# A two-block kernel under a new written order: every engine's queue, the buffer slots and the filler matmuls exchanged

## The chip, the cores and the metric

The kernel runs on one core of a Trainium2 chip. A core has TensorE (matrix products into the accumulator memory PSUM; "PE" in the profile, its weight loads "PEld"), VectorE (DVE), ScalarE (ACT), GpSimd (POOL) and SyncE (SP), which here only issues DMA transfers; ScalarE and GpSimd issue some too. Every engine works through its own queue strictly in the written order and waits at semaphores for the others. The metric is the device time of one execution in microseconds (us); lower is better.

## The reference

Attention with sketched polynomial features for 4 batches, 4 heads, 1088 tokens and head size 32, and then a token-mixing block over the heads joined to 128 channels:

```python
a, b = einsum('rd,bhsd->bhsr', S1, x), einsum('rd,bhsd->bhsr', S2, x)
phi(x) = einsum('bhsi,bhsj->bhsij', a, b)              # 8 x 8 = 64 features
num = phi(q) @ (phi(k)^T v);  den = phi(q) @ sum(phi(k)) + 1e-06
x = num / den                                          # joined: (4, 1088, 128)
theta = x @ w_theta;  zr, zi = x * cos(theta), x * sin(theta)
u = x + w_tok_r @ zr + w_tok_i @ zi                    # w_tok_*: 1088 x 1088
out = u + maximum(u @ w_ch, 0)
```

## The kernel before

The kernel does not issue its work in the order in which its source describes it. The source declares 1022 operations, numbered 0 to 1021 in the order of the calls of `op` (`vop`, `small` and `join` call it too). Each names its engine ("P" TensorE, "V" VectorE, "A" ScalarE, "G" GpSimd, "S" SyncE), what it reads and writes, and holds a function that issues one or many instructions. `Layout.run` then takes the order from the string `ORDER`, a permutation of the 1022 numbers, and a slot for every buffer from the string `PLACES`. `Layout.issue` issues them one after the other, so an engine's queue is the subsequence of `ORDER` that belongs to it. `SPINS` says ahead of which operations how many filler matmuls go (`spin`, line 379: 384 columns of zeros, into a bank that nobody reads). The classes of buffers are in the table `classes`: 22 big ones, 5 of class "zs" for raw weight rows and for z, 8 PSUM banks, and smaller ones. Two buffers in the same slot follow one another: the first operation of the later one waits for all users of the earlier one. All waits follow from the data and the slots.

The stages, with the numbers that the text uses (b is the batch, g a group of three 128-token chunks, of which each batch has three):

- *Start*: fillers (1), constants (2), a dummy sine `warm` (3, line 384), the sketch matrices and their scaling (5 to 43; 7 is ScalarE's Prelu at line 412, 16 its scaling at lines 469 to 471, 17 VectorE's rounding; 41 and its GpSimd products 42 and 43 belong to a product of the two sketches; 31 builds the blocks that the first product of the chain takes). Loads on SyncE: k 44, 47, 48, 49, q 45, 50, 51, 52, v 46, 53, 54, 55 for batches 0 to 3, a second copy of k for batches 2 and 3 (56, 57), and w_theta with w_ch (58).
- *Keys and chain* (58 to 304): transposes of k, features, outer products on VectorE and products with v (of batch 2, the third outer product is 207 and its product 208), a Gram matrix of k, and a chain of tiny operations that makes scales and sliced feature matrices.
- *Queries* (305 to 334): transposes and slices of q; 328 and 329 are the correction of batch 2's q, which GpSimd adds by an accumulating DMA.
- *Weight rows* (335 to 419): 17 rows of 128 x 1088 eight-byte words arrive in "zs" slots and are unpacked: five operations a row, a load (SyncE), two activations (ScalarE, lines 584 and 586), a shift and an addition (VectorE, lines 309 and 305). Row i has the numbers 335 + 5i to 339 + 5i; row 13's addition is 404 and row 16's 419.
- *Per batch* (420 on): "levels" (products of q with the feature matrices, lines 987 to 1005), "den" (VectorE), "num" (outer product, transposition, product, copy into xT), "theta" (products with w_theta; ScalarE turns the phase with lines 1111 to 1117, three of which are Abs and two sines; VectorE subtracts at line 312 and multiplies into z at line 305). For batches 2 and 3 transpositions go through memory: VectorE turns blocks of 32, SyncE and ScalarE scatter them (line 333), SyncE fetches them back.
- *Mixing*: batch 0 takes all three column spans of a row in one operation (482 to 498, row 16 in 498), batch 1 one span at a time (579 to 641). Batches 2 and 3 share seven half-size products, `winograd` (787 to 1006), which need sums of weight rows (line 305, 128 x 544) and differences of z (835 for the first). Then the output product and the store.

In theta of batch 0, 468 and 460 are VectorE's subtractions for groups 1 and 0, 459 is ScalarE's copy ahead of 460, and 469 to 471 are the Abs and the two sines of group 1. In theta of batch 2, 695 and 717 are VectorE's products into z of groups 0 and 2; 815 and 793 are the first matmuls that need them. The num products of batch 3 are 740, 747 and 754; the scatters that ScalarE issues for it are 738, 745 and 752.

Of the kernel before, what the change touches and what calls it, by code (L numbers as in the profile page):

```python
# [26 lines left out]
TINY = 2.0**-60  # L27
UP = 256.0
ORDER = (
# [37 lines left out]
)  # L67
PLACES = (
# [8 lines left out]
)  # L77
SPINS = (
    "70:2 15:3 137:1 211:1 424:2 128:1 168:1 174:2 176:1 521:2 "
)  # L80
WARM = 0
SPLIT = ()
# [1330 lines left out]
```

## Time and profile before

| | |
|---|---|
| median of 3 runs (lowest, highest) | 219.07 us (218.96, 219.25) |
| profiled execution, first to last instruction | 217.4 us; the page gives no other time of it |
| TensorE busy | 209.3 us (96%), 1998 matmuls |
| VectorE busy | 181.2 us (83%) |
| ScalarE busy | 111.2 us (51%) |
| GpSimd busy | 22.2 us |
| DMA | 40.58 MB, mean 187 GB/s; over 290 GB/s in most of the first 100 us |
| granted TensorE clock | 0.997 of full speed |

Busy times are unions of rows, and the rows of matmuls overlap in the pipeline: a row of 0.27 us can be followed by the next after 0.11 us. Where an operation's price is meant, the time from start to start says more. An engine that is not the bottleneck may stand idle at no cost, so what matters is which engine has no room in which stretch of the span.

### The profile page before, as it was taken

What the parts mean: (1) busy time and instruction counts of PE and PEld (TensorE: products, weight loads), DVE (VectorE), ACT (ScalarE), POOL (GpSimd) and SP (SyncE); (2) the same over time, 40 slices, a digit from 0 to 9 for tenths busy, and PEclk for the clock granted to TensorE, in tenths of its full rate; (3) what the DMA queues carried; (4) which work ended last, traced back from release to release, by engine and by line L of the source; (5) the groups of instructions that cost most, each with busy time, mean ns of one, the idle gap of its engine ahead of it and who ended that gap; (6) DMA issues with size and microseconds to landing.
All of it is one profiled execution on the core that took longest, in us unless ns stands there. A gap on an engine that the chain in (4) does not pass through costs nothing.

```text
span 217.4 us, 5063 instructions
## 1 busy us (share of the span) xinstructions
PE 209.3 (96%) x1998; PEld 154.3 (71%) x1998; DVE 181.2 (83%) x408; ACT 111.2 (51%) x214; POOL 22.2 (10%) x44
## 2 busy tenths in 40 slices
PE   7999899999999999999999999999999999999994
PEld 3987786686766686666766575667758788888883
DVE  4899999999999999999599839988138999996542
ACT  3998498899779999983322040354037400000010
POOL 2237000055000000100132000100101000000000
PEclk9999999999999999999999999999999999999998
DMA  5999996869979979894226998599911000045253
GB/s 153 429 406 340 425 399 203 333 224 271 267 276 361 361 264 380 219 198 126 33 36 102 222 137 199 105 156 151 231 78 32 0 0 0 3 66 89 36 79 75
DMA packets 52635, 40.58 MB, mean 187 GB/s; under 512 B 45444, under 2 KB 47108, under 8 KB 50436
## 3 DMA queue, kind: packets, MB, share of 16 engines
q1 hardware_dynamic: 35540, 33.71, 48.7%
q0 software_dynamic: 1728, 4.65, 10.5%
q10 hardware_dynamic: 15344, 1.90, 6.0%
q8 instruction: 15, 0.25, 0.5%
q14 instruction: 8, 0.07, 0.1%
HBM read 30.43 MB, written 5.18 MB: 164 GB/s over the span
## 4 chain that ended last, share of the span: by engine, by line
PE 72%; DVE 12%; ACT 8%; DMA 4%; ACTq 2%; issue 2%; SPq 1%
PE ps L341 66%; DMA big<-q_l 2%; DVE lv L305 2%; PE ps L1064 2%; ACTq L333 2%; PE ps L1098 1%; DMA fx<-g 1%; DVE g L305 1%; DVE big L305 1%; PE ps L967 1%; ACT big L584 1%; ACT big L937 1%; DVE hf L309 1%; DVE zs L305 1%; ACT g L1068 1%
## 5 line engine op out<-in xcount | busy, mean ns | idle before, releaser
L341 PE MATMUL ps<-big,zs 128*128 128x384 f32 (+4 forms) x398 | 109.7, 424 | 0.4 <-DVE zs L305 0.4
L341 PEld LDWEIGHTS ps<-big,zs 128*128 128x128 f32 x398 | 71.4, 190 | 30.3 <-issue 2.6
L1201 ACT COPY g<-ps 128x128 f32<-128x128 f32 (+1 forms) x3 | 0.9, 301 | 42.5 <-PE ps L1193 42.5
L305 DVE CUSTOM_DVE_ANT_0 big<-big,big 128x2176 uint16<-128x2176 uint16 x17 | 21.8, 1287 | 0.4 <-ACT big L586 0.2
L584 ACT ACTIVATE big<-zs 128x1088 f32<-128x1088 f32 x17 | 20.9, 1235 | 2.1 <-DMA zs<-w_tok 1.2
L586 ACT ACTIVATE big<-zs 128x1088 int32<-128x1088 uint32 (+1 forms) x18 | 21.3, 1184 | 0.1
L341 PE MATMUL ps<-big,big 128*64 128x64 f32 (+2 forms) x208 | 20.6, 276 | 0.0
L341 PEld LDWEIGHTS ps<-big,big 128*64 128x64 f32 (+1 forms) x208 | 16.5, 154 | 2.9 <-issue 0.2
L305 DVE TENSOR_TENSOR big<-big,big 128x544 f32<-128x544 f32 x24 | 16.7, 712 | 0.0
L1002 ACT COPY lv<-ps 128x480 f32<-128x480 f32 x12 | 6.3, 563 | 14.2 <-PE ps L341 14.2
L312 DVE SCALAR_TENSOR_TENSOR g<-g,ps 128x384 f32<-128x384 f32 x12 | 6.6, 548 | 8.1 <-ACT g L1111 8.1
L1078 ACT COPY big<-ps 128x384 f32<-128x384 f32 x12 | 5.9, 489 | 14.0 <-PE ps L341 8.3
L309 DVE TENSOR_SCALAR big<-big 128x1088 int32<-128x1088 int32 x17 | 12.2, 724 | 0.6 <-ACT big L584 0.5
L341 PEld LDWEIGHTS ps<-w,big 128*128 128x128 f32 x80 | 10.6, 192 | 2.3 <-ACT g L1068 0.6
L319 POOL DMA_DIRECT2D big<-hf x6 | 5.4, 957 | 63.3 <-DVE g L312 33.8
L319 POOL DMA_DIRECT2D g<-big x6 | 5.2, 920 | 64.8 <-ACT g L1179 34.7
L341 PE MATMUL ps<-w,big 128*128 128x128 f32 x80 | 11.8, 280 | 0.0
L305 DVE TENSOR_TENSOR g<-lv 128x768 f32<-128x768 f32 x12 | 11.2, 945 | 0.0
L341 PE MATMUL ps<-g,sm 128*64 128x384 f32 x48 | 10.1, 507 | 0.2 <-ACT big L1078 0.2
L305 DVE TENSOR_TENSOR zs<-ps,g 128x768 f32<-128x768 f32 (+2 forms) x15 | 9.4, 632 | 1.0 <-PE ps L1098 0.9
L341 PEld LDWEIGHTS <-hf 128*64 128x64 f16 (+1 forms) x288 | 7.7, 110 | 2.9 <-issue 1.7
L379 PE MATMUL ps<-idle 128*128 128x384 bf16 x27 | 7.8, 400 | 1.3 <-POOL idle L381 1.3
(194 smaller groups left out, 336.6 us busy)
## 6 DMA issues: line engine op xcount, KB each, us to landing
zs<-w_tok SPq DMA_DIRECT2D x17, 1088.0 KB, 7.0
big<-k_l SPq DMA_DIRECT2D x6, 576.0 KB, 6.6
big<-hf POOLq DMA_DIRECT2D x6, 576.0 KB, 6.0
big<-v_l SPq DMA_DIRECT2D x4, 576.0 KB, 7.0
g<-fq SPq DMA_DIRECT2D x6, 384.0 KB, 5.2
big<-q_l SPq DMA_DIRECT2D x3, 576.0 KB, 5.1
fq<-g SPq DMA_DIRECT2D x12, 96.0 KB, 4.0
fq<-g ACTq DMA_DIRECT2D x12, 96.0 KB, 4.1
```

Source lines behind the costliest of these rows:

```text
L305: eng.tensor_tensor(out=o, in0=a, in1=b, op=f)
L309: (eng or V).tensor_scalar(out=o, in0=a, scalar1=s1, scalar2=s2, op0=op0, **kw)
L312: (eng or V).scalar_tensor_tensor(out=o, in0=a, scalar=s, in1=b, op0=op0, op1=op1)
L319: op("G", 0.9, lambda: G.dma_start(dst(), src(), accum_op=ALU.add), w, r, fly=fly)
L333: E.dma_start(there().rearrange("(a i) (x b j) -> b i x a j", a=nf, b=nf, j=SQ)[f], blocks()[f * SQ:(f + 1) * SQ].rearrange("i (x a j) -> ...
L341: T.matmul(o, lhs, rhs, start=start, stop=stop, skip_group_check=True)
L379: T.matmul(nowhere() if home is None else view(home, (GW,), F32), idle()[:, 0:P], idle(), start=True, stop=True, skip_group_check=True)
L584: op("A", 0.22 + n * 0.0009, lambda: A.activation(dfn(), words_of(raw(), n)[1].bitcast(F32), AF.Prelu, scale=2.0**-112, alpha=-(2.0**32)), ...
L586: op("A", 0.22 + n * 0.0009, lambda: A.activation(stp(), words_of(raw(), n)[0].bitcast(U32), AF.Copy, scale=2.0**-29), [stp], [raw])
L1002: op("A", act(480), lambda g=g, lp=lp: A.copy(lv().rearrange("p l (c n) -> p l c n", n=HR)[:, :, g * GC:(g + 1) * GC], lp().rearrange("p c ...
L1064: T.transpose(tr()[:, i * P:(i + 1) * P], qp()[:, i * H + 2 * n:i * H + 2 * n + 2].rearrange("p h i j -> p (h i j)"), ident())
L1078: op("A", act(GW), lambda g=g, xp=xp: A.copy(xt()[:, g * GW:(g + 1) * GW], xp()), cells(xt, g * GW, (g + 1) * GW), [xp])
```

## The change

Three strings are exchanged, `ORDER`, `PLACES` and `SPINS`. The operations, their functions and all that is computed stay the same, and so does the number of buffer slots of each class. What differs is the sequence of every engine's queue, which buffers share a slot, and where how many fillers go. The diff, cut to the lines of the new strings that the text speaks of (the old `ORDER` begins with the two lines shown):

```diff
 ORDER = (
-    "6 4 2 5 44 0 1 45 50 3 47 7 340 8 48 46 11 9 10 49 12 29 58 13 30 70 83 84 64 76 71 14 77 85 96 15 88 72 89 78 "
-    "65 86 90 97 79 16 91 66 159 17 92 26 87 98 67 148 27 93 80 32 18 68 19 73 99 309 25 94 141 20 310 74 95 31 142 "
...
+    "4 5 6 7 2 8 9 44 11 10 0 1 12 70 13 83 14 15 71 47 64 16 129 58 84 85 88 89 65 135 29 30 45 26 17 18 90 130 131 66 "
+    "49 21 148 151 40 41 43 132 50 59 61 91 152 92 48 136 153 133 93 19 86 149 96 150 97 94 95 20 159 355 98 87 101 67 "
+    "60 102 305 99 306 160 161 340 103 137 162 138 68 104 22 23 72 73 154 246 25 74 42 309 310 31 105 139 307 36 35 106 "
...
+    "354 387 518 216 520 437 438 523 465 524 525 217 439 453 467 254 255 468 147 440 454 386 256 199 441 469 526 470 471 "
+    "241 527 528 529 455 188 200 456 360 189 442 530 531 361 532 466 242 533 457 459 460 51 473 475 257 267 540 536 218 "
...
+    "404 495 569 556 416 417 243 649 557 294 558 559 418 419 299 496 497 3 498 295 296 560 511 512 499 561 625 626 505 "
...
 SPINS = (
-    "70:2 15:3 137:1 211:1 424:2 128:1 168:1 174:2 176:1 521:2 "
+    "70:1 113:1 233:2 126:1 448:2 189:2 536:2 "
 )
```

Read by engine: SyncE's queue begins with 6, 44, 45, 50, 47, 340, 48, 46, 49, 58 before, and with 6, 44, 47, 58, 45, 49, 50, 48, 355, 340 after. The dummy sine 3 is ScalarE's second entry before; after, it follows the second sine of theta in batch 1, group 0 (559), behind the unpacking of row 16 (416, 417). The last two weight rows in VectorE's queue are 13 and 16 after; they were 15 and 16 before. The fillers of the first product (operation 1, ten of them) and the one of operation 128 stay.

80 rows, old and new, of tables (ORDER, PLACES) are left out of this document.

## The prediction

> **What bounds the kernel now.** First the table of busy time by stretch of the span (start:end and length in us, then busy us and instructions of TensorE, its weight loads, VectorE, ScalarE and GpSimd, the granted clock, the DMA engines' share, GB/s).
>
> ```profile
> 0.00:24.00 24.00, 21.94 (x367) 17.27 (x367) 19.77 (x83) 19.24 (x48) 8.58 (x29) 1.00 0.88 341
> 24.00:60.00 36.00, 34.17 (x595) 26.20 (x595) 35.69 (x88) 30.45 (x59) 5.95 (x5) 1.00 0.89 296
> 60.00:100.00 40.00, 39.34 (x311) 26.64 (x311) 38.85 (x66) 36.13 (x56) 0.85 (x1) 1.00 0.86 280
> 100.00:145.00 45.00, 44.71 (x396) 28.71 (x394) 35.66 (x73) 11.92 (x24) 5.10 (x7) 1.00 0.66 126
> 145.00:170.00 25.00, 24.91 (x118) 18.66 (x119) 15.25 (x30) 11.65 (x25) 1.71 (x2) 1.00 0.57 120
> 170.00:200.00 30.00, 30.00 (x134) 24.82 (x133) 28.24 (x55) 0.87 (x2) 0.00 (x0) 1.00 0.16 26
> ```
>
> From 24 to 100 us VectorE is busy for 74.5 of 76 us: nothing can be put in there. From 100 us on it has room (35.7 of 45, 15.3 of 25) and TensorE has none. Then VectorE's waits between 24 and 102 us, which are all that the view lists:
>
> ```profile
> DVE big L309 <- ACT big L584: 0.5, 2, 0.3
> DVE big L305 <- ACT big L586: 0.2, 1, 0.2
> ```
>
> So there are two stages: until the last token-mixing row is unpacked VectorE sets the pace, and afterwards TensorE works off what is left. The hinge shows in the timeline (start, length, instruction; the last unpacking on VectorE) and in the chain that ended last (TensorE's long pieces):
>
> ```profile
> 98.63 1.29 DVE L305 CUSTOM_DVE_ANT_0 big<-big,big 128x2176 uint16<-128x2176 uint16 x1
> ```
>
> ```profile
> 83.10 44.99 PE ps L341 x362
> ...
> 145.07 21.94 PE ps L341 x102
> ...
> 172.89 37.32 PE ps L341 x170
> ```
>
> Last the rows of two things that the change moves, from the groups (busy us, mean ns, then the idle time ahead and what ended it):
>
> ```profile
> L379 PE MATMUL ps<-idle 128*128 128x384 bf16 x27 | 7.8, 400 | 1.3 <-POOL idle L381 1.3
> L384 ACT ACT_TABLE_LOAD x1 | 1.3, 1283 | 1.6 <-DVE hm L366 1.6
> ```
>
> **How I count.** An operation's price is the time from its start to the next start on its engine, where that one waited for nothing (rows overlap by some 0.1 us, so row lengths would count too much). Added so, VectorE has 181.2 us of work, ScalarE 127 with its DMA issues, and TensorE 198.2 without fillers. A filler between others starts 0.163 us ahead of the next. Adding the prices in the written order gives the work that stands ahead of each operation in both kernels; clock time less this sum is what an engine has lost.
>
> Before: up to the end of row 16's unpacking (operation 419) VectorE has 94.9 us of work; the clock says 99.92, so 5.0 are lost, 3.0 of them by 13.7 us, while the first loads arrive, and the rest in drips. Its matmuls (498) start at 100.18. From there TensorE has 111.1 us of work and ends at 213.98: 2.7 lost, of which 0.45 is the wait for zs at 144 us and the rest switches between kinds of matmul, 0.05 to 0.1 us each. The last instruction ends 3.4 us later: 100.2 + 111.1 + 2.7 + 3.4 = 217.4, the span. The page gives no other time of the profiled execution; the median of the runs, 219.07, is 1.67 above the span, and I carry that over.
>
> **The change, part by part.** No operation comes or goes, so nothing is won from work except fillers: 16 become 11, 5 x 0.163 = 0.8 us. Those of before stand partly in waits, and so do the new ones (ahead of 113, 448, 189 and 536, each of which waits for VectorE), so the saving lies between 0 and 0.8; it is contained in the TensorE sums below.
>
> *Which VectorE operation is the last that TensorE must wait for.* In the new order it is the outer product 207 (batch 2, third group): VectorE's work up to its end is 86.5 us, and TensorE's work from its user 208 to the end is 121.3. Together 207.8, against 94.9 + 111.1 = 206.0. Nearly as tight is row 13 (404 for 495: 91.7 + 116.0 = 207.7). So the new order holds TensorE back at a point where it has 10 us more to do: +1.8 us.
>
> *The start.* On SP's queue k of batch 1 moves from fifth to third, ahead of both q, and row 1 behind k of batches 2 and 3. Before, k0 landed at 5.36, q0 at 7.15, q1 at 8.57 and k1 at 9.99, so k1 should land at about 7 and q0 at 9.2. The scaling of the small matrices (16, 17), late by ScalarE's place in the queue (8.8 us), follows k0's first copy at 6.6. Following VectorE's queue with these times I find nothing it waits for between 6 and 24 us, and a loss of 2.1 at 14 us in place of 3.0: -0.9 us. Bounds: 0 (the load comes no earlier) and -1.5. The drips (1.7 us from 14 to 87 us) I leave as they were. POOL's queue has the small product 43 ahead of the slices; it waits for 41 at about 10.4, and what is behind it (31, wanted at 15.9) ends at about 13.4.
>
> *The table load.* Operation 3, the dummy sine, goes from the head of ScalarE's queue to row 16's end. The one load row stands ahead of it, and it is the kernel's first function. The new first function is the Prelu of 7, and the first sine is 470 (theta, batch 0, group 1). Whether a Prelu's table holds a sine no row shows: a second load costs ScalarE between 0 and 1.28 us, and I take 1.28, as the one load that shows belongs to a sine. Does VectorE feel it? 469 ahead of it waits for VectorE's 468. From 469 to the end of 459 ScalarE has 4.7 us of work; VectorE, from the end of 468 to 460, which needs 459, has 4.9. With the load, 6.0 against 4.9: VectorE stands for 1.1 us, in the full stage and ahead of 207. Without it the cover is 0.2.
>
> [...]
>
> *Behind 100 us.* The three num products of batch 3 (740, 747, 754) now follow each other, which saves about two pairs of switches, 0.4 us; the 0.45 wait should go, as 695 ends some 1.4 us ahead of 815. But theta2_2 now ends just as its user 793 is due (both at about 154), behind ScalarE's scatter issues for batch 3 (738 and 752: 2.2 and 1.3 us on ScalarE), and zc1 (835) ends 0.3 us ahead of 846. For these I take 0.5 us (0, if they hold, to 2, if the issues are as slow as the slowest pair, 3.5 us). 2.7 - 0.4 - 0.4 + 0.5 = 2.4.
>
> *Slots.* Row 16's raw slot is freed by row 12's second activation (397) at about 89.7; with its 7.0 us to land, ScalarE has it at 96.7, and VectorE wants it at 98.4. The q2 correction (POOL, 329) leaves at 81 and lands in 6.3 us; its user 652 is due at 88.9. Covers of 1 to 2 us: no cost, and all of a delay beyond them.
>
> Sum: 86.5 + (2.1 + 1.7 + 1.1 lost) + 121.3 + 2.4 + 3.4 = 218.5, 1.1 above 217.4; 219.07 + 1.1 = **220.2 us**.
>
> **Rivals.** (1) *Faster: VectorE loses less ahead of 207.* If ScalarE keeps a lead over VectorE all along (at 460 too), the start's 2.1 and 0.5 of drips remain, 2.6 instead of 4.9: 216.2, or 217.9 in the runs. For it: the waits above, the only ones listed for the full stage, are for ScalarE's unpacking (0.7 us), and by the sums the new order has that unpacking 8 to 10 us of VectorE work earlier. Against: the cover of 0.2 at 460. It decides below a loss of 3.8. (2) *No second load, or it is covered:* 217.4, no change, 219.1. For it: ScalarE has idle time; against: the count above. (3) *A load or a round trip is late* at one of the covers of 1 to 2 us: row loads took up to 11 us among others (row 13), 4 more than I allow, so 2 to 3 us more: 222.5.
>
> **Chances.** Forecast 0.48, rival 1 0.28, rival 2 0.1, rival 3 0.14. 0.2% (0.4 us) is about what these runs can tell from no change. Of the forecast's share a little falls within that, of rival 2's a third on each side: faster 0.33, same 0.12, slower 0.55. Alone the forecast has 219.3 to 221.3. The range takes in rival 1's 217.9 with 1.2 us for more of the start and the fillers, and rival 3's 222.5: 216.7 to 222.6.
>
> **What the profile after would show.** A second ACT_TABLE_LOAD row at about 49 us on ScalarE, and VectorE waiting for L1111 some 1 us there: if the row is absent, that step is wrong. k1 landed near 7 us and VectorE's work 0.9 us further at 14 us. TensorE waiting for VectorE at L341 (kv, batch 2) near 91 us, and 498 starting after 101. Waits for zs (theta2_2) near 154 would show the tight second stage. I am wrong if VectorE shows other waits of a microsecond between 24 and 95 us, or none.

## The result, and the profile after

The changed kernel takes 226.38 us (median of 4 runs, 225.89 to 228.12), against 219.16 us for the kernel before beside it: 1.0324 times as long, 95% interval 1.0274 to 1.0374. The forecast was 220.2 us, the range ended at 222.6. The profiled execution spans 224.5 us, 7.1 more than before.

First the page's line of busy times and the head of its chain that ended last, for the kernel after:

```profile
PE 210.2 (94%) x1993; PEld 153.6 (68%) x1993; DVE 185.8 (83%) x408; ACT 113.8 (51%) x215; POOL 21.7 (10%) x44
...
DVE 49%; PE 36%; issue 7%; ACT 6%; POOL 1%; DMA 1%; DVEq 0%; POOLq 0%; ACTq 0%
```

The same line of the kernel before:

```profile
PE 72%; DVE 12%; ACT 8%; DMA 4%; ACTq 2%; issue 2%; SPq 1%
```

There TensorE carried most of the chain; now VectorE carries half of it. VectorE's busy time has grown by 4.6 us, from 181.2, with the same 408 instructions. The table by stretch of the kernel after (columns as in the prediction):

```profile
24.00:60.00 36.00, 30.40 (x590) 23.17 (x591) 33.70 (x85) 30.55 (x59) 4.10 (x5) 1.00 0.79 258
60.00:100.00 40.00, 38.98 (x398) 27.20 (x399) 39.01 (x73) 34.62 (x54) 1.77 (x2) 1.00 0.78 281
100.00:145.00 45.00, 44.68 (x312) 28.00 (x311) 36.95 (x69) 16.37 (x31) 3.90 (x5) 1.00 0.66 132
```

Still two stages, VectorE's and then TensorE's, but the first ends later. The waits of VectorE between 24 and 102 us in the kernel after are again all that this view lists:

```profile
DVE g L310 <- ACT g L1109: 0.4, 1, 0.4
DVE sm L303 <- PE ps L339: 0.4, 1, 0.4
```

So the page shows an engine that is late and waits for nobody. Where TensorE meets it is where the prediction put it: the timeline of TensorE after (start, length, instruction, then the idle time ahead and its releaser) has operation 208, the user of 207, waiting for VectorE:

```profile
97.43 0.54 PE L339 MATMUL ps<-g,big 128*32 128x64 f32 x24 [0.53 <-DVE g L303]
```

From there the sum of the prediction holds to 0.1 us: 97.43 + 121.3 of work + 2.5 lost behind it + 3.3 for the tail = 224.5. All of the error lies ahead of this point. 207 ends at 97.38, and its sum of work is the forecast's 86.5: VectorE has lost 10.9 us on the way, where I had 4.9.

**Where a VectorE that waits for nothing loses 6 us.** The same kind of instructions take the same time in both kernels. The groups' rows of the kernel before (busy us, mean ns of one, then the idle time ahead):

```profile
L305 DVE CUSTOM_DVE_ANT_0 big<-big,big 128x2176 uint16<-128x2176 uint16 x17 | 21.8, 1287 | 0.4 <-ACT big L586 0.2
L305 DVE TENSOR_TENSOR big<-big,big 128x544 f32<-128x544 f32 x24 | 16.7, 712 | 0.0
```

And the same rows of the kernel after:

```profile
L303 DVE CUSTOM_DVE_ANT_0 big<-big,big 128x2176 uint16<-128x2176 uint16 x17 | 21.9, 1288 | 0.8
L303 DVE TENSOR_TENSOR big<-big,big 128x544 f32<-128x544 f32 x24 | 16.6, 709 | 1.2 <-PE ps L339 1.0
```

All VectorE rows added, the lengths differ by 0.2 us between the kernels. What differs is where a row starts against the end of the one ahead. From the timeline of VectorE after:

```profile
83.98 0.72 DVE L307 TENSOR_SCALAR big<-big 128x1088 int32<-128x1088 int32 x1
84.73 1.29 DVE L303 CUSTOM_DVE_ANT_0 big<-big,big 128x2176 uint16<-128x2176 uint16 x1
85.94 0.17 DVE L307 TENSOR_SCALAR mv<-sm 128x32 f16<-128x32 f32 x1
```

The unpacking (84.73) reads what the shift ahead of it (83.98 to 84.70) writes, and starts 0.03 behind its end. The third row reads something else and starts 0.08 ahead of the end of the second (86.02). Taken over all pairs of neighbouring operations up to 419, an operation that reads its predecessor's result starts 34 to 35 ns behind that one's end (median, in both kernels) and any other 82 to 84 ns ahead of it. A neighbour that depends so costs 0.118 us more. One operation in between is enough: those that read the result of the last but one start some 83 ns ahead, like the independent ones. Before has 10 dependent neighbours up to 419 (9 up to 207), after has 65 (63 up to 207): 54 x 0.118 = 6.4 us at 207. The page counts none of it as idle; it shows only in the busy time, a union of rows, from which the overlaps have gone.

What in the engine sets the two values apart, the traces do not show; they give the +35 and -83 ns alone.

### The profile page after: what moved, and what is told of

Same layout as the page of the kernel before. It is cut to its first block, busy times and chain, and to the rows that moved or that the text cites. A ratio compares the mean times of both kernels' runs of the same rounds, so it can differ in the third digit from the quotient of the medians.

```text
span 224.5 us, 5068 instructions
## 1 busy us (share of the span) xinstructions
PE 210.2 (94%) x1993; PEld 153.6 (68%) x1993; DVE 185.8 (83%) x408; ACT 113.8 (51%) x215; POOL 21.7 (10%) x44
## 4 chain that ended last, share of the span: by engine, by line
DVE 49%; PE 36%; issue 7%; ACT 6%; POOL 1%; DMA 1%; DVEq 0%; POOLq 0%; ACTq 0%
PE ps L339 35%; DVE big L303 12%; DVE g L303 7%; DVE big L307 5%; DVE zs L303 4%; DVE hf L307 3%; DVE lv L303 3%; DVE sm L310 3%; DVE sm L303 2%; DVE g L310 2%; DVE sm L307 2%; DVE big L310 1%; ACT big L582 1%; POOL sg L303 1%; DMA st<-s 1%
## 5 line engine op out<-in xcount | busy, mean ns | idle before, releaser
L339 PE MATMUL ps<-big,zs 128*128 128x384 f32 (+4 forms) x398 | 107.9, 423 | 0.7 <-DVE zs L303 0.7
L339 PE MATMUL ps<-w,big 128*128 128x128 f32 x80 | 11.1, 276 | 0.0
L1109 ACT ACTIVATE g<-ps 128x384 f32<-128x384 f32 x12 | 5.7, 485 | 10.6 <-DVE big L303 6.0
L377 PE MATMUL ps<-idle 128*128 128x384 bf16 x22 | 6.7, 416 | 3.3 <-ACT big L753 1.8
L310 DVE SCALAR_TENSOR_TENSOR g<-ps,g 128x384 f32<-128x384 f32 (+3 forms) x9 | 4.2, 463 | 6.4 <-PE ps L339 6.0
```

What stands on the lines that cost most here:

```text
L310: (eng or V).scalar_tensor_tensor(out=o, in0=a, scalar=s, in1=b, op0=op0, op1=op1)
L339: T.matmul(o, lhs, rhs, start=start, stop=stop, skip_group_check=True)
L377: T.matmul(nowhere() if home is None else view(home, (GW,), F32), idle()[:, 0:P], idle(), start=True, stop=True, skip_group_check=True)
L1109: op("A", act(GW), lambda cs=cs, th=th: A.activation(cs()[:, 0], th(), AF.Copy, bias=ROUND), [(cs, 0)], [th])
```

## The experiments

Theory N: the dependent neighbours on VectorE. Theory S: the start and the two table loads. Theory T: TensorE's own order. Theory C, added later: the granted clock. All ratios are to runs of before in the same comparison (medians 219.5 to 219.7 us).

### More dependent neighbours in the kernel before

VectorE's order alone, 49 of its 347 operations moved, none to more than seven places from where it stood; an excerpt of its queue (428 to 430, 164 to 166 and 432 to 434 each read the one ahead):

```diff
-427 349 428 319 429 127 164 62 165 430 166 431 249 432 169 433
+348 349 428 429 430 319 127 62 249 164 165 166 431 432 433 434
```

> The kernel before with VectorE's operations alone moved, each by at most six places, so that more of them stand directly behind the operation whose result they read: up to operation 419 67 such neighbours instead of 10. One table load, start, slots, fillers and TensorE's order are those of before. Theory N: 57 x 0.118 = 6.7 us more on VectorE ahead of 419, of which 6.0 to 6.7 reach TensorE: span 217.4 + 6.3 = 223.7, time about 225.4, without any listed wait of VectorE having grown. Theory S and theory T: nothing of what they blame is in this kernel: 219.1 within 0.5.

Measured: 226.72 us, ratio 1.0346 (1.0286 to 1.0406), as slow as the changed kernel, with nothing of its table loads, slots, start or TensorE order. 419 ends at 107.42, against 99.92 in before. As the granted clock had fallen in three slices, the order was run again with more fillers in TensorE's waits:

```diff
-    "70:2 15:3 137:1 211:1 424:2 128:1 168:1 174:2 176:1 521:2 "
+    "70:2 15:3 137:2 211:1 424:2 128:1 168:9 174:2 176:1 521:2 105:2 135:4 422:6 158:4"
```

> The paired order of before once more (67 neighbours that read their predecessor's result, 10 in before, up to operation 419), with 25 more fillers in the waits that TensorE had in it up to 44 us, as the granted clock fell to 0.72 and 0.69 in three slices of that run. Theory N: the clock had little to do with the 7.2 us, since VectorE sets the pace there: 225.4 to 227. Theory C (clock): the slow clock made them, and with a clock of 1.0 the kernel is at 221 or below.

Measured: 225.68 us, ratio 1.0271 (1.0235 to 1.0306), clock 1.0, span 224.3. 419 ends at 107.00: 7.1 us later than in before, where 57 x 0.118 gives 6.7. Between 24 and 108 us the view of waits lists one wait of VectorE:

```profile
DVE big L306 <- ACT lv L999: 1.0, 1, 1.0
```

The time is 1.0 to 1.6 us below the first run's (by medians and by ratios), but the two intervals overlap, so what the clock had cost there is not told apart from nothing. Two timelines of VectorE show the edit; first that of the kernel before:

```profile
31.44 0.75 DVE L312 SCALAR_TENSOR_TENSOR big<-lv 128x576 f32<-128x576 f32 x1
32.11 0.76 DVE L309 TENSOR_SCALAR hf<-big 128x1152 f16<-128x1152 f32 x1
32.78 0.75 DVE L305 TENSOR_TENSOR lv<-big 128x576 f32<-128x576 f32 x1
```

Then that of the paired order with more fillers:

```profile
34.79 0.75 DVE L309 SCALAR_TENSOR_TENSOR big<-lv 128x576 f32<-128x576 f32 x1
35.58 1.43 DVE L302 TENSOR_TENSOR lv<-big 128x576 f32<-128x576 f32 x2
36.92 0.75 DVE L306 TENSOR_SCALAR hf<-big 128x1152 f16<-128x1152 f32 x1
```

In before the conversion to hf stands between the writer of big and its reader, and each starts 0.08 to 0.09 ahead of the end of the row above it (31.44 + 0.75 = 32.19). In the paired order the reader follows its writer and starts 0.04 behind the end (35.54). Theory N stands; S and T, which expected 219.1, and C, which expected 221 or below, fall as the main cause.

### Fewer dependent neighbours in the changed kernel

VectorE's order alone, 39 operations moved by a few places:

```diff
-343 344 358 38 359 172 426 427 175 251 125 428 429 430 177 178
+343 171 358 344 359 172 426 125 427 175 251 428 429 177 430 178
```

> The changed kernel with VectorE's operations alone moved, each by a few places, so that fewer of them stand directly behind the operation whose result they read (up to operation 207: 18 such neighbours instead of 63, up to 419: 19 instead of 65); every other engine's order, the slots and the fillers stay. Theory N (neighbours): in the trace of after, an instruction on VectorE that reads its predecessor's result starts 35 ns behind that one's end, an independent one 83 ns ahead of it, so each such neighbour costs 0.118 us; 45 fewer are worth 5.3 us at 207, of which TensorE should see 4.5 to 5.3: span 224.5 - 4.9 = 219.6, time about 221.5. Theory S (start and table loads): the lost time comes from the first table load standing behind a transfer and from the second at 54.7 us, and VectorE would wait for ScalarE anyway: the gaps turn into waits, time 226 within 1. Theory T (TensorE): TensorE's own order holds the end: no change either, 226.

Measured: 224.02 us, ratio 1.0204 (1.0159 to 1.0248), 1.2% of 219.5 or 2.6 us less than the changed kernel; the span falls by 3.0, and so does the end of 207 (94.34). The direction is N's, the size only 3.0 of 5.3. Most of the rest came back as waits; VectorE between 24 and 105 us, in the kernel with the spread order:

```profile
DVE sm L311 <- PE ps L340: 0.8, 1, 0.8
DVE big L308 <- ACT lv L1001: 0.6, 1, 0.6
DVE sm L308 <- PE ps L340: 0.6, 2, 0.3
DVE g L311 <- ACT g L1110: 0.4, 1, 0.4
DVE big L304 <- ACT big L585: 0.2, 1, 0.2
```

That is 2.6 us where the changed kernel has 0.8, so 1.8 of the 2.3 that did not come; the other 0.5 stays open. A VectorE that gets ahead arrives before its inputs: the neighbours' time had partly hidden other lateness.

### The sine and the table loads

In the changed kernel the constants and the dummy sine go back to the head:

```diff
-    "4 5 6 7 2 8 9 44 11 10 0 1 12 70 13 83 14 15 71 47 64 16 129 58 84 85 88 89 65 135 29 30 45 26 17 18 90 130 131 66 "
+    "4 5 6 2 3 7 8 9 44 11 10 0 1 12 70 13 83 14 15 71 47 64 16 129 58 84 85 88 89 65 135 29 30 45 26 17 18 90 130 131 66 "
...
-419 299 496 497 3 498
+419 299 496 497 498
```

> The changed kernel with the constants (2) and the dummy sine (3) put ahead of 7, so that the one table load is again under way while the first transfers fly. Theory N: the second load goes and the first no longer stands behind the transfer (0.73 us of VectorE's start); VectorE's wait of 0.5 at 460 goes: 0.6 to 1.2 us less, 225.2 to 225.8. Theory S: most of the 7.2 us goes: 220 to 222.

Measured: 225.06 us, ratio 1.0245 (1.0224 to 1.0266), 1.7 us less than the changed kernel by the ratios and 1.3 by the medians; span and the end of 207 fall by 1.2 and 1.3. Both edits together:

> Both edits. Theory N: the gains add, and the sine's is somewhat larger, as VectorE has less slack to give: 221.5 less 0.6 to 1.7, 220.3. Theory S: the same as the sine's edit alone, 220 to 222, and the spread adds nothing to it.

Measured: 222.71 us, ratio 1.0158 (1.0121 to 1.0195), span 220.6: the sine adds 0.9 to the spread's 3.0. The same move the other way round, in the kernel before (the sine alone, to behind 419):

```diff
-6 4 2 5 44 0 1 45 50 3 47 7
+6 4 2 5 44 0 1 45 50 47 7
...
-419 288
+419 3 288
```

> The kernel before with the dummy sine (3) alone moved, to behind row 16's last unpacking (419), as the change has it; everything else is that of before. Two table loads are expected, one behind the transfer of s at the start and one ahead of the first sine (theta, batch 0, at about 56 us). Theory N (both loads are small terms): 0.7 us at the start, of which VectorE's later wait for the first loads may take some back, and 0 to 1.3 us at theta: 219.5 + 0.6 to 1.9. If the second load is worth the 1.1 us that the prediction gave it, the sum of both is 1.8; if VectorE's lead over ScalarE covers it, 0.6. Theory S (the loads are most of the 7.2 us): 222 or more.

Measured: 220.20 us, ratio 1.0033 (1.0018 to 1.0048), 0.7 us; its span is 218.6, 1.2 more. The groups' rows of this kernel show the two loads:

```profile
L411 ACT ACT_TABLE_LOAD x1 | 1.3, 1283 | 2.4 <-DMA st<-s 2.4
...
L1114 ACT ACT_TABLE_LOAD x1 | 1.3, 1283 | 0.0
```

The second load is there, and the first now starts at 2.40, behind the transfer of s instead of beside it, which makes VectorE 0.7 us late at operation 8. By 10 us 0.15 of that is left; 0.5 comes at 21 us, where VectorE waits for TensorE (operation 112), and 0.9 at theta, some of which VectorE makes good before 419 (1.1 later than in before). Worth 0.7 to 1.7 us by kernel, the loads are a real term, but a small one.

### The fillers, and the clock

```diff
-    "70:1 113:1 233:2 126:1 448:2 189:2 536:2 "
+    ""
```

> The changed kernel without its 11 fillers. They stand in waits of TensorE and the granted clock is 0.998 with them. Theory N: no change, 226.4 within 0.5. A rival (theory F): the new fillers cost TensorE their 0.163 us each, 1.8 us in all: 224.6. Another: without them the clock falls in the first 60 us and the time rises.

Measured: 227.21 us, ratio 1.0334 (1.0296 to 1.0371): no change that can be told. In the trace the clock was 0.72 from 24 to 30 us. The traced execution took 225.62 us at a mean clock of 0.991; the other three had 0.977 to 0.984 and took 227.2. Of the changed kernel's four, one had 0.976 and took 228.12, and three had 0.998 or 0.999 and took 225.89 to 226.47. So a lower clock went with some 1.6 us more in both kernels. That the fillers hold it up fits this, but with four executions each it is not shown.

### Orders searched with these prices

If the prices were complete, a search with them should find better orders. 141 of TensorE's 357, 134 of VectorE's 347 and 95 of ScalarE's 214 operations moved, and some of GpSimd's and of SyncE's loads too, from before:

```diff
-    "6 4 2 5 44 0 1 45 50 3 47 7 340 8 48 46 11 9 10 49 12 29 58 13 30 70 83 84 64 76 71 14 77 85 96 15 88 72 89 78 "
+    "6 4 2 5 44 0 1 45 50 3 340 7 8 11 9 12 10 70 13 84 76 83 71 29 14 85 64 77 30 47 15 48 88 86 72 65 78 96 89 16 "
...
```

> The kernel before with the same slots and fillers and an order searched from it by moving single operations, priced by the traces: a VectorE or ScalarE operation that reads its predecessor's result starts 0.118 or 0.135 us later than one that doesn't, TensorE pays 0.02 us for each change of kind, and a finished transfer counts from its measured flight. Theory N, whose prices these are: 219.5 less 1 to 4.8 us (4.8 is the sum by these prices; what hangs on single transfers may not come). If the prices leave out what matters, the time is that of before or above it, as it was with the changed kernel.

Measured: 230.68 us, ratio 1.0532 (1.0468 to 1.0595), the slowest of all, with 9 dependent neighbours up to 419. One reason is in the table by stretch of this kernel:

```profile
12.00:15.00 3.00, 1.72 (x22) 1.35 (x20) 1.53 (x4) 2.41 (x7) 0.00 (x0) 1.00 1.03 416
15.00:18.00 3.00, 3.00 (x34) 2.53 (x35) 2.43 (x12) 2.80 (x5) 1.16 (x4) 0.52 0.98 393
18.00:21.00 3.00, 3.00 (x28) 2.04 (x27) 2.83 (x6) 1.63 (x4) 2.92 (x6) 0.50 0.65 196
21.00:24.00 3.00, 2.66 (x27) 2.29 (x29) 0.95 (x1) 2.02 (x8) 1.05 (x5) 0.84 0.98 334
```

After 3 us with TensorE busy for only 1.72, the granted clock is 0.52 and 0.50 for the next 6 us. How little work lowers it is not shown: in the changed kernel 1.86 of 3 us (9 to 12 us) left the clock at 1.00 up to 24 us. With 23 more fillers in TensorE's waits:

```diff
-    "70:2 15:3 137:1 211:1 424:2 128:1 168:1 174:2 176:1 521:2 "
+    "70:2 15:3 137:3 211:1 424:2 128:1 168:2 174:5 176:1 521:2 141:4 95:6 105:3 135:2 111:2"
```

> The searched order of before, which was 11 us slower than before while its prices promised 4.8 less, with 23 more fillers in the waits that TensorE had in it up to 38 us. There the granted clock was 0.50 to 0.52 from 15 to 21 us, and TensorE and VectorE lost some 4 to 5 us against the sum by 24 us. Theory C: the clock is what the search did not price; with it held, those 4 to 5 us come back, and more where loads were pushed: 225 to 226, clock 1.0. If the fillers hold the clock and the time stays at 230, the order itself is what is slow; if the clock stays low, fillers in waits do not hold it.

Measured: 229.28 us, ratio 1.0434 (1.0398 to 1.0469), clock 0.998. The fillers hold the clock, and that gives back 1.4 us of 11, not the 4 to 5 expected. The order itself is slow: VectorE loses 10.2 us up to 419 (before: 4.9), TensorE 5.7 behind 498 (before: 2.7). Most of that is in listed waits that the prices had not foreseen: VectorE's up to 419 come to 8.1 us (before: 3.4), TensorE's behind 100 us to 1.8 (before: 0.4). The stretch from the last matmul's end to the end of the span grew as well, from 3.2 to 5.1 us. Which of the moves does it was not tested. The same search from the changed kernel with its order spread and the sine first; 122, 150 and 81 operations moved (TensorE, VectorE, ScalarE), beginning:

```diff
-    "4 5 6 2 3 7 8 9 44 11 10 0 1 12
+    "4 5 6 2 3 7 8 9 44 11 0 1 12 70
...
```

> The same search started from the changed kernel with its VectorE order spread and the sine first, with the changed kernel's slots and fillers. By the same prices it lies 1.2 us above the other searched order, and 3.5 below before: 216 to 219.5. If the new slots themselves hold the kernel back, it stays at 222 or above.

Measured: 225.73 us, ratio 1.0288 (1.0254 to 1.0322), with 15 dependent neighbours and the clock at 0.50 from 24 to 30 us: 3.0 us above the kernel that the search started from (222.71, 19 neighbours). So the slots aren't shown to hold it back, nor cleared.

Last, two small edits of before. VectorE alone, nine operations moved (273 beside the eight that the expectation names), of which this is the place at 144 us:

```diff
-838 304 742 708 743 702 695 749 750 706
+838 304 742 702 743 708 695 749 750 706
```

> The kernel before with eight VectorE operations moved by a few places behind 22 us (38, 460, 523, 327, 394, 408, and 702 with 743 ahead of 742), so that TensorE's wait for zs at 144 us (0.45 us) goes and three short waits shrink; TensorE's and ScalarE's orders, slots and fillers are those of before. By the prices of the traces 0.4 to 1.7 us less: 219.5 - 0.7 = 218.8. If TensorE's other losses fill it up, no change.

Measured: 220.98 us, ratio 1.0060 (1.0042 to 1.0077): slower. In its trace (of the slowest of 13 executions, 222.43 us) 702, moved ahead, stood waiting for its own input for 1.6 us, and TensorE, which was to gain 0.45 at 815, waited 1.3 us there. With 15 operations of VectorE and 15 of ScalarE moved:

```diff
-838 304 742 708 743 702 695 749 750 706
+838 304 742 743 749 708 695 702 750 756
...
```

> The same with ScalarE's operations moved too, 31 operations in all, none of them a transfer. By the same prices 2.2 us less than before, of which 0.5 to 2 may come: 217.5 to 219. If ScalarE's order lets TensorE's clock fall or an operation late, above before.

Measured: 219.24 us, ratio 0.9982 (0.9963 to 1.0001): not told apart from before. None of these orders beats the kernel before beyond doubt.

## Why the prediction was wrong

What VectorE has lost at the start of 419, and how many dependent neighbours stand ahead of it, read off the traces in the way of the prediction (clock less the sum of the prices):

| kernel | neighbours up to 419 | lost, us | span, us |
|---|---|---|---|
| before | 10 | 4.9 | 217.4 |
| after | 65 | 11.2 | 224.5 |
| before, paired, more fillers | 67 | 12.0 | 224.3 |
| after, spread | 19 | 8.2 | 221.5 |
| after, sine first | 65 | 10.0 | 223.3 |
| after, spread, sine first | 19 | 7.3 | 220.6 |

**The step that failed** is "The drips (1.7 us from 14 to 87 us) I leave as they were". They became 7.2 us: 3.6 were lost by operation 133 at 14 us, 10.8 when 207 starts. Of these 57 x 0.118 = 6.7 us are dependent neighbours, since 63 stand ahead of 207 and 6 of them by 133. The way of counting hid them: a price from start to start belongs to a pair of neighbours, and I gave it to the operation alone. Before's own rows showed both values, +35 and -83 ns, and the two orders gave the number of pairs.

**The start** was a gain of 0.9 us in the forecast and a loss of 0.6 by the clock at 14 us. k1 landed at 6.95, as forecast, but nothing at that point waited for it: the load of the first table behind the transfer (the step counted only the second) and 0.4 us of waiting for TensorE at operation 41 came in its place.

**The second table load** came at 54.70 with 1283 ns, ahead of 470, and VectorE waited at 460: right in kind. The wait cost 0.5 us (0.4 in the view, and the overlap that it took away) and not 1.1: between 468 and 460 VectorE has three operations that read the result just ahead, which made its way 0.4 us longer than the 4.9 of the forecast, and ScalarE took 5.7 us, not 6.0. That VectorE was late as a whole did not matter: with the order spread it comes to 460 2.4 us earlier, and the wait is 0.4 again. In this timeline of ScalarE in the kernel after, the load takes its 1.28 us, with gaps of 0.02 and 0.01 us around it:

```profile
54.16 0.52 ACT L1112 ACTIVATE g<-g 128x384 f32<-128x384 f32 x1
54.70 1.28 ACT L1113 ACT_TABLE_LOAD   x1
55.99 0.61 ACT L1113 ACTIVATE g<-g,halfpi 128x384 f32<-128x384 f32 x1
```

The load starts 0.02 us behind the end of the row ahead, and the next function 0.01 behind it.

**Right:** that TensorE's last long wait for VectorE is 208 for 207, with 121.3 us of work behind it; that 2.4 us are lost behind it (2.5), and that the wait for zs at 145 goes while theta2_2 (717 for 793) is tight (TensorE lost 0.1 there); that fewer fillers win nothing; and that no cost of the slots or of the joins of q shows (no wait of VectorE from 24 to 102 us is for a DMA). Rival 3, a load or round trip too late, did not happen. The forecast took "or none" as a sign that it is wrong, and that was the sign: no listed wait of a microsecond in that stretch, and yet 6 us.

The sum as it should have stood: 86.5 of work at 207, plus 4.9, plus 54 x 0.118 = 6.4, gives 97.8 for its end, against 97.38 measured. That it comes so close is in part luck: the start lost 1.5 us more than the 2.1 of the forecast, and drips and second table load, neighbours aside, 0.5 instead of 2.8.

How much of the 7.1 us is the later meeting point itself (1.8 in the prediction) was not tested alone. By the sums the 7.1 are these 1.8 and 5.9 of VectorE's loss ahead of the meeting point (10.9 against 5.0), less some 0.6 in small changes behind it. It agrees with the kernel that has both edits: 19 neighbours, one table load, and still 3.2 us of span above before.

## What to carry to other kernels

Price neighbours, not operations: on an engine that sets the pace, as VectorE does here up to 100 us, count the places where an instruction reads the result of the one just ahead, and put something independent in between; on VectorE it was 0.118 us a time, and more than 50 of them. They did not show as waits: look for a busy time that grows while every group's mean stays, and for rows that no longer overlap. And in orders as tight as these the inputs come just in time: here prices from a trace gave the cost of the added neighbours to within 0.4 us, but neither the searches nor the small edits that went by them gave an order that is faster beyond doubt.

## What was not expected of the hardware

- On VectorE the start of a row stands 83 ns ahead of the end of an independent predecessor and 35 ns behind that of one whose result it reads; on ScalarE the medians are about 0.1 us ahead and 32 to 33 ns behind. On VectorE one operation in between brings back the overlap.
- The granted clock fell to about half for several microseconds in some of the new orders (0.52 and 0.50 from 15 to 21 us in the searched one), in the paired one too (0.55 from 40 to 42 us), where TensorE's own order is that of before; 23 and 25 more fillers in TensorE's waits held it at 0.998 and 1.0.
- A table load moved behind a transfer was seen at operation 8 as 0.7 us, of which 0.15 was left at 10 us; the load moved ahead of theta cost more, 0.9 us there.
